# Cosine attention and a Hyena gate: k and v on 112 partitions of five tokens, and the last output rows of two batches in one tile

## The chip, the cores and the metric

The kernel runs on one core of a Trainium2 chip, in one launch. The metric is device time in microseconds (us): the median of several executions, beside one execution that a hardware profiler recorded. Inputs and outputs lie in device memory in fp32; inside, most tiles are fp16 with sums in fp32.

Engines are named as in the profile: PE (TensorE, matrix products) with its weight loads PEld, DVE (VectorE), ACT (ScalarE), POOL (GpSimd) and SP (SyncE, which here only issues DMA transfers). Each engine has a queue of its own and works it off in order; engines wait for each other through semaphores.

## The reference, cut to what matters

```python
# q, k, v: (8, 8, 576, 64) = batch, heads, sequence, head_dim
theta = pi/2 * arange(S) / S
phi(x) = concat(relu(x) * cos(theta), relu(x) * sin(theta))      # along head_dim
kv  = einsum('bhsf,bhsd->bhfd', phi(k), v)
z   = phi(k).sum(axis=2)
num = einsum('bhsf,bhfd->bhsd', phi(q), kv)
den = einsum('bhsf,bhf->bhs', phi(q), z)[..., None] + 1e-6
x   = (num / den).transpose(0, 2, 1, 3).reshape(B, S, 512)

x1, x2, x3 = split(x @ w_proj, 3)                                # w_proj (512, 1536)
conv = irfft(rfft(x2, axis=1) * rfft(filter)[None], n=S)          # filter (576, 512)
out  = (x1 * conv * x3) @ w_out                                  # w_out (512, 512), fp32
```

Attention needs sums over all 576 tokens of a head, in any order: `kv` and `z` do not depend on which token lies in which partition, as long as `k`, `v` and the angle columns agree. The output product, by contrast, needs its rows in a known order, since they are stored to their places.

## The kernel before, in words

**Tiling.** 576 is 4.5 x 128, so the tokens of a batch are dealt over 128 partitions and five columns (`NJ = 5`). `load_rows` (L156) does it with two transfers: tokens 0 to 511 go as four consecutive ones to each of 128 partitions, a run of 1 KB (L158), and the last 64 tokens as one each to partitions 0 to 63, a run of 256 B (L163). In the fifth column partitions 64 to 127 hold nothing; they are set to zero once per buffer. There are six raw buffers (`raw_buf`), used in turn by q, k and v of each batch: buffer (3 b + 0, 1 or 2) modulo 6. So 1 and 4 hold k, 2 and 5 hold v, 0 and 3 hold q. `step_pad` (L234, words `pad0` to `pad5`) zeroes their empty parts on DVE; `step_cols` (L242, word `cols`) does it for two more buffers, `k32` and `v32`.

**Loads.** `step_load` (L167, words `Lq`, `Lk`, `Lv`) issues them on POOL's queue and converts to fp16 on the way. The first four heads of k and v of batch 0 come in fp32 over SP's queue instead (`step_load32`, L174, words `Sk`, `Sv`). A word with a tilde, `~Lq3.1`, makes the load wait for the newest DVE instruction and the newest DMA transpose ahead of it in the plan (`hold`, L148).

**Attention, per batch.** `pk` (L505) makes phi(k) in ten instructions per batch or half batch, one for each column and for cosine and sine, each on ACT (L514) or DVE (L111). Its scales are the columns `ccol` and `scol`, cosine and sine of the angle of the token in each place, which `step_cols` makes from an index tile `s4_i` (L205). `pq` (L519) makes phi(q) with the cosine divided out, so that only one column `tcol` (the tangent) is needed; `epsc` is the matching small term. `va` (L539) copies v beside a column of ones. `kv` (L556, matmul L563) sums over the partitions and, in five accumulating matmuls per head, over the columns. `qt` (L573) turns phi(q): by PE for batches 0 and 1, by a DMA transpose on SP's queue from batch 2 on (L577). `num` (L600, matmul L606) multiplies by `kv`, and DVE divides (`rcp`, `att`).

**Gate, per batch.** `fx` (L629) takes a Fourier-like step of the attention result; `xt` (L659) turns that result, from batch 3 on by one DMA transpose on SP's queue (L660); `pr` (L676, matmul L680) projects to x2 in the frequency domain, and its evictions from PSUM (the accumulator memory) are the `x2f` instructions; `dft` (L701) and `mul` (L718) apply the filter; `ga` and `gb` (L730, matmul L736) are the projections to x1 and x3; `g` (L751) multiplies those two; `inv` (L765, matmuls L770 and L774) goes back to time.

**The end of a batch.** `y` (L786) adds and subtracts halves and multiplies by `g`. A step `y3.0.2` treats two of the four channel blocks (`NC = 4`) of batch 3, from block 0. Its last instruction writes `ye`, the gated values of the last 64 rows (L811 to L817); a batch that runs in two such steps has written `ye` after the second, and one that runs in more after the last. `out` (L837) multiplies by `w_out`. Groups 0 and 1 are two tiles of 128 rows each, matmul L824, one eviction of 128x1024 (`os`) and two stores (L850). Group 2 is the last 64 rows: to use all 128 output partitions, `out_tile` computes the two column halves into partitions 0 to 63 and 64 to 127, in two matmuls of 64x256 for each channel block (L829); `left` (L853) evicts 128x256 on ACT and stores the two halves on SP's queue (L858). The last batch goes by `end` (L863) in single tiles.

**What sets the order.** Nothing is scheduled automatically. One long string of words, the plan (L905 to L987), is carried out word by word while the program is built. A word names a step, its batch and its part; a step is a generator that yields after each piece, and every occurrence of its word emits one more piece, `*3` three of them. `'a` and `'v` put a piece on ACT or DVE. Each engine executes its share of what the plan emits, in the plan's order. For `out*.2` the pieces are: the matmuls; the eviction; the two stores.

PSUM is used through `unit`, a pool of four buffers taken in turn. The tiles around the end of a batch have `y` and `ye` two buffers each, `os` three and `os4` one.

Where the words of the last rows stand in the plan before (each `...` leaves out other words):

```
... fx3.0 out0.2 ... y1.0.2 ... pr4.0 ... out1.2*2 pr4.2 out1.2 ...
... y2.0.2 ... fx5.3 fx5.2 out2.2 fx5.3 ... y3.0.2 gb5.1 ga4.3 out3.0 ... inv5.1 out3.2 qt7.2 ...
... dft7.1'v dft7.0 xt7 dft7.2 out5.1 ga7.0 inv6.3 dft7.2'v gb7.0 out4.2 ... gb7.0 out5.2 mul7 ...
```

Of the kernel before, what the change touches and what calls it, by code (L numbers as in the profile page):

```python
# [17 lines left out]
def kernel(  # L18
# [41 lines left out]
    NM = NC * 128  # L60

# [104 lines left out]

    def step_load(nm):  # L167
        def load(b, half):
            raw_t[(b, nm)] = raw_buf[(3 * b + "qkv".index(nm)) % len(raw_buf)]
            load_rows(nc.gpsimd, raw_t[(b, nm)], {"q": q, "k": k, "v": v}[nm], b, at(half))  # L170
            yield
        return load

    def step_load32(nm):  # L174
        def load(b, half):
            load_rows(nc.sync, k32 if nm == "k" else v32, k if nm == "k" else v, b, at(half))
            yield
        return load
# [26 lines left out]
    def step_iota(part):  # L205
        if part == 0:
            iota("s4_i", [128, NJ], lambda t: [
                (t[:, 0:4], [[1, 4]], 0, 4), (t[0:64, 4:5], [[1, 1]], NM, 1),
                (t[64:128, 4:5], [[1, 1]], 0, 1),
            ])  # L210
            yield
            return
# [21 lines left out]
    def step_pad(i):  # L234
        nc.vector.memset(raw_buf[i][64:128, :, 4 * D : 5 * D], 0.0)
        yield
# [5 lines left out]
    def step_cols():  # L242
        nc.vector.memset(warm, 0.0)
        nc.vector.memset(half_pi, PI / 2.0)
        for r in (k32, v32):
            nc.vector.memset(r[64:128, :, 4 * D : 5 * D], 0.0)
        yield
        nc.scalar.activation(
            out=ccol, in_=cc["s4_i"], func=AF.Sin, scale=-(PI / 2.0) / S, bias=half_pi
        )  # L250
        nc.scalar.activation(out=scol, in_=cc["s4_i"], func=AF.Sin, scale=(PI / 2.0) / S)
        yield
# [5 lines left out]
        nc.vector.reciprocal(out=epsc, in_=ccol)  # L258
        yield
        nc.vector.tensor_tensor(out=tcol, in0=epsc, in1=scol, op=AL.mult)  # L260
# [244 lines left out]
    def step_pk(b, half):  # L505
# [4 lines left out]
        for j in range(NJ):  # L510
            for x, col in enumerate((ccol, scol)):
                dst, src, c = kp_t[b][:, j, hs, x], rw[:, hs, ds(j * D, D)], col[:, j : j + 1]
# [26 lines left out]
    def step_va(b, x):  # L539
        n = 2 if b == 0 else 4  # L540
        hs = slice(n * x, n * x + n)
        ev(
            va_buf[b % 2][:, hs, :, 0:D],
            (v32 if b == 0 and x < 2 else raw_t[(b, "v")])[:, hs].rearrange(
                "p h (j d) -> p h j d", j=NJ
            ),
        )
        yield
# [7 lines left out]
    def step_kv(b, half):  # L556
# [3 lines left out]
        for g in range(hv.start, hv.stop):  # L560
            for h in range(4 * g, 4 * g + 4):
                for j in range(NJ):
                    nc.tensor.matmul(  # L563
                        u[:, g, ds((h % 4) * 65, 65)], kp[:, j, h].rearrange("p a b -> p (a b)"),
                        va[:, h, j, 0:65], start=(j == 0), stop=(j == NJ - 1),
                    )
# [219 lines left out]
    def step_y(b, c, n):  # L786
# [24 lines left out]
        if "ye" not in moe[b]:  # L811
            moe[b]["ye"] = late["p"].tile([128, NC, 64], FP16, tag="ye", bufs=2, name=f"ye{b}")
        tt(
            out=moe[b]["ye"][:, c : c + n].rearrange("p c (a t) -> p c a t", t=4),
# [5 lines left out]
    def out_tile(b, t, dst, cs):  # L820
        y = moe[b]["y"]
        for c in cs:
            if t < 4:
# [3 lines left out]
                continue  # L827
            for hf in range(2):
                nc.tensor.matmul(  # L829
                    dst[ds(64 * hf, 64), 0 : DM // 2], moe[b]["ye"][:, c],  # L830
# [22 lines left out]
    def left(b, u):  # L853
        os_ = late["p"].tile([128, DM // 2], FP32, tag="os4", bufs=1, name=f"os{b}_4")
# [35 lines left out]
    def run(plan, **batch):  # L890
# [27 lines left out]
        tf'v pk1.2*4 qt1.0 va1.0'v kv1.2 va1.1'v kv1.2 th kv1.2 qt1.1 g0.0.2 qt1.0'v th
        ~Lq3.1 tf qt1.0'v qt1.1'v qt1.2 qt1.1'v qt1.2 ~Lk3.0 qt1.2 num1.0*3 tf pr0.1 th
        num1.1 num1.0 num1.2 g0.2.2 num1.1 tf ~Lq3.0 num1.2 num1.1 pr0.1 tf ti pr0.0 num1.2  # L920
        num1.1 qt1.3 num1.2 pr0.0 pr0.2 qt1.3 dft0.0 feo0 pr0.2 dft0.0 feo1 h0 qt1.3'v xp1.0
        ti xp1.0 pq2.2 fx1.1 pq2.2 h0'v h1 ~Lv2.2 pq2.2 xp1.0 pq2.2 pk2.2 xp1.0'v pk2.2
        pk2.2'a h0 fx1.1 pk2.2 num1.3*3 pq2.2 num1.3 pq2.2 qt2.3 h2 qt2.0 fx1.2 h1 pk2.2 h1
        pk2.2 xp1.1 fx1.3 xp1.1 ~Lk3.1 ~Lq4.1 ~Lv3.1 h2 fx1.2 xp1.1'v fx1.3 xp1.1'v fx1.0
        pk2.2*2 dft0.1 dft0.1'v ~Lo dft0.2 ga1.0 fx1.0 dft0.2 mul0 ti mul0 pr1.0 pr1.2 ti*2
        mul0 ga1.0 mul0 pr1.1 pr1.1'v pr1.0 ga1.0 inv0.1 inv0.0 ~Lq4.0 ti pk2.2 late pr1.2
        dft1.2 dft1.0 dft1.2'v inv0.1 dft1.1 pk2.2 inv0.0 inv0.2 va2.0'v dft1.0 kv2.2 pq3.2
        va2.1'v inv0.3 kv2.2 y0.0.2 ~Lk4.1 y0.0.2 dft1.1 inv0.2 ga1.2*2 mul1 gb1.2 mul1
        qt2.1 kv2.2 num2.0 ~Lv3.0 qt2.2 num2.0 inv0.3 num2.1 pq3.2'a ga1.2 gb1.2 ~Lv4.0
        num2.1 num2.0 num2.1 num2.0 num2.1 gb1.3*2 mul1*2 gb1.2 gb1.1*2 pq3.2'a pq3.2 gb1.3  # L930
        pq3.2'a ga1.1 pk3.2 gb1.1 num2.2 ~Lk4.0 num2.2*3 y0.0.2 ga1.1 y0.0.2 fx2.1 y0.2.2
        ga1.1 y0.2.2 gb1.0*2 pk3.2'a fx2.1 inv1.1 fx2.2 pk3.2 gb1.0 inv1.1 fx2.2 ga1.3
        y0.2.2 ga1.3 inv1.0 inv1.0'v ga1.3 xp2.0 num2.3*3 xp2.0*3 num2.3 pk3.2 inv1.3*2
        y0.0.2 inv1.2*2 fx2.0*2 fx2.3*2 g1.0.2 ga2.0 xp2.1*2 pr2.0 xp2.1*2 pq3.2 ga2.0
        y0.2.2 qt3.0 va3.0'v y1.0.2 pk3.2 pk3.2'a*2 pk3.2 y0.2.2 pk3.2'a pq4.2 pr2.1 ga2.0
        qt3.2 pq4.2 out0.0 pr2.2 pr2.1 pr2.0 out0.0 dft2.1 y1.0.2 dft2.0 ~Lq5.0 va3.1'v
        y1.0.2 ~Lq5.1 ~Lv4.1 y1.0.2 pk3.2 ~Lv5.0 qt3.1 y1.2.2*2 pr2.2'v dft2.1 y1.2.2 dft2.2
        kv3.2*2 y1.0.2 gb2.1 y0.2.2 gb2.1 dft2.0 g1.2.2 y0.0.2 pq4.2'a ~Lv5.1 qt3.3 dft2.2'v
        kv3.2 gb2.0*2 mul2*2 num3.0*4 ~Lk5.0 gb2.1 gb2.0 gb2.3 pk4.2'a gb2.3*2 ~Lk5.1 out0.2
        ga2.2*2 fx3.0 out0.2 pq4.2'a ga2.1 mul2*2 ga2.2 fx3.0 num3.1*2 num3.2*2 pk4.2'a  # L940
# [78 lines left out]
```

## Time and profile before

| | |
|---|---|
| time, median of 3 executions | 223.5 us (222.74 to 224.11) |
| the profiled execution: its own time | 224.69 us |
| the same, span from first to last instruction | 222.9 us |
| mean granted PE clock in it | 0.983 |
| read from memory, written | 33.69 MB, 9.44 MB (193 GB/s over the span) |
| DMA packets, and those under 512 B | 90907, 58944 |

The page gives the span once more in 40 slices of 5.57 us, in tenths of the slice:

```profile
PE   7388989999999999999999999799999999999990
...
DVE  7998999989999989989999997889888797589930
```

The largest groups of instructions:

| group | count | busy us | mean ns |
|---|---|---|---|
| PE, gate projections, L736 | 512 | 71.2 | 286 |
| PE, x2 projection, L680 | 160 | 34.6 | 381 |
| PE, output rows, L824 | 128 | 30.1 | 379 |
| DVE, `att` from `num` and `rcp`, L116 | 32 | 26.0 | 819 |
| ACT, `os` from `out` (groups 0 and 1, last rows), L138 | 24 | 18.3 | 767 |
| POOL, loads of q, k and v, L158 | 40 | 32.2 | about 804 |

How to read it: busy time is a sum over instructions, and matmuls overlap, so the mean of one is longer than the pace at which they follow each other. An idle time of an engine is put down to the instruction or transfer that ended it ("releaser"). In rows of a stage the columns are the stretch in us, its length, then for PE, PEld, DVE, ACT and POOL the busy time and in brackets the instructions, then the granted PE clock, the mean share of DMA engines in use and the GB/s they moved. In rows of the timeline they are the start, the busy time from first to last of the instructions put together, the engine (with a q for its DMA queue), line and operation, what is written and read, the count, and in square brackets the idle time before and what ended it.

### The profile page before, as it was taken

How to read it: one execution, taken by the hardware profiler on the slowest of the kernel's cores; microseconds unless marked ns; L12 is line 12 of the kernel's file. 1: busy time of each engine (PE TensorE's matmuls, PEld its weight loads, DVE VectorE, ACT ScalarE, POOL GpSimd, SP SyncE). 2: the span in 40 equal slices, each digit the busy share in tenths (PEclk: the TensorE clock that was granted, in tenths of full speed). 3: DMA queues.
4: the chain of work that ended last, by engine and by line, in shares of the span. 5: the costliest groups of instructions: out<-in, count | busy, mean ns of one | idle time of the engine just before them, and what ended most of it. 6: DMA issues, size and time to landing. Idle time of an engine off the chain costs nothing.

```text
span 222.9 us, 5869 instructions
## 1 busy us (share of the span) xinstructions
PE 207.7 (93%) x2316; PEld 142.8 (64%) x2316; DVE 194.7 (87%) x473; ACT 170.7 (77%) x275; POOL 65.5 (29%) x105
## 2 busy tenths in 40 slices
PE   7388989999999999999999999799999999999990
PEld 2176776574888476756686667476876667477630
DVE  7998999989999989989999997889888797589930
ACT  4796989998898999888784975877787736476651
POOL 8892456213962096003500184002200000000000
PEclk9979999999999999999999999999999999999996
DMA  5999999999999999999999999997999940823084
GB/s 170 190 186 192 191 209 193 175 138 210 144 189 184 173 161 182 169 195 163 170 157 194 200 199 182 146 300 156 110 177 149 326 132 3 197 94 138 22 258 165
DMA packets 90907, 38.39 MB, mean 172 GB/s; under 512 B 58944, under 2 KB 86592, under 8 KB 90880
## 3 DMA queue, kind: packets, MB, share of 16 engines
q0 software_dynamic: 38944, 16.26, 59.8%
q1 hardware_dynamic: 51568, 21.17, 46.0%
q10 hardware_dynamic: 368, 0.59, 0.7%
q8 instruction: 18, 0.29, 0.5%
q14 instruction: 9, 0.07, 0.1%
HBM read 33.69 MB, written 9.44 MB: 193 GB/s over the span
## 4 chain that ended last, share of the span: by engine, by line
PE 67%; DVE 14%; DMA 10%; ACT 3%; issue 2%; POOL 2%; ACTq 0%; DVEq 0%; POOLq 0%
PE x L736 22%; PE x L680 11%; PE out L824 10%; DMA xt<-att 4%; PE kv L563 4%; PE num L606 4%; PE dft L711 3%; PE fx L634 3%; DMA out_dram<-os 3%; DMA raw<-in_q_dram 3%; PE inv L770 3%; PE inv L774 2%; DVE kp L111 2%; DVE yf L116 2%; DVE qp L111 2%
## 5 line engine op out<-in xcount | busy, mean ns | idle before, releaser
L736 PE MATMUL x<-xt,wp 128*128 128x288 f16 x512 | 71.2, 286 | 0.6 <-DMA xt<-att 0.3
L736 PEld LDWEIGHTS <-wp 128*128 128x128 f16 x512 | 47.9, 98 | 15.8 <-issue 2.8
L680 PE MATMUL x<-wp,fx 128*128 128x512 f16 (+1 forms) x160 | 34.6, 381 | 0.0
L824 PE MATMUL out<-wo,y 128*128 128x512 f16 x128 | 30.1, 379 | 0.0
L138 ACT ACTIVATE os<-out 128x1024 f32<-128x1024 f32 (+2 forms) x24 | 18.3, 767 | 12.5 <-PE out L824 10.1
L116 DVE TENSOR_TENSOR att<-num,rcp 128x640 f16<-128x640 f32 x32 | 26.0, 819 | 0.6
L680 PEld LDWEIGHTS <-fx 128*128 128x128 f16 (+1 forms) x160 | 13.6, 100 | 15.0 <-issue 2.1
L138 ACT CAST x0s<-x 128x576 f16<-128x576 f32 x27 | 17.2, 641 | 6.0 <-PE x L736 5.1
L138 ACT CAST x2s<-x 128x576 f16<-128x576 f32 x28 | 17.8, 639 | 4.8 <-PE x L736 4.7
L138 ACT ACTIVATE x2f<-x 128x1024 f16<-128x1024 f32 (+1 forms) x18 | 16.2, 903 | 6.6 <-PE x L680 5.6
L158 POOL DMA_DIRECT2D raw<-in_q_dram x14 | 11.2, 797 | 31.4 <-ACT x0s L138 18.2
L824 PEld LDWEIGHTS <-y 128*128 128x128 f16 x128 | 12.1, 98 | 12.6 <-issue 0.4
L138 ACT CAST fx<-fx 128x576 f16<-128x576 f32 x29 | 17.8, 648 | 1.8 <-PE fx L640 1.5
L138 ACT CAST eq<-inv 128x576 f16<-128x576 f32 x26 | 16.0, 648 | 3.9 <-PE inv L774 3.3
L158 POOL DMA_DIRECT2D raw<-in_k_dram x13 | 10.5, 811 | 27.0 <-DVE rcp L617 14.6
L770 PE MATMUL inv<-itab,yf 128*128 128x144 f16 x128 | 16.9, 226 | 1.2 <-ACT x2f L138 0.9
L158 POOL DMA_DIRECT2D raw<-in_v_dram x13 | 10.5, 805 | 21.8 <-DVE rcp L116 17.3
L774 PE MATMUL inv<-itl,yf 128*128 128x288 f16 x64 | 16.8, 286 | 0.0
L563 PE MATMUL kv<-va,kp 128*128 128x65 f16 x320 | 12.4, 193 | 4.0 <-DVE va L134 3.8
L563 PEld LDWEIGHTS <-kp 128*128 128x128 f16 x320 | 11.6, 98 | 5.8 <-ACT kp L514 4.0
L606 PEld LDWEIGHTS <-qpt 128*128 128x128 f16 x320 | 13.0, 98 | 3.6 <-issue 0.9
L606 PE MATMUL num<-kvs,qpt 128*128 128x65 f16 x320 | 14.3, 194 | 0.9 <-ACT qpt L138 0.5
(163 smaller groups left out, 432.8 us busy)
## 6 DMA issues: line engine op xcount, KB each, us to landing
out_dram<-os SPq DMA_DIRECT2D x30, 256.0 KB, 3.2
raw<-in_q_dram POOLq DMA_DIRECT2D x12, 256.0 KB, 6.9
raw<-in_k_dram POOLq DMA_DIRECT2D x11, 256.0 KB, 7.2
raw<-in_v_dram POOLq DMA_DIRECT2D x11, 256.0 KB, 6.5
wp<-in_moe_w_proj_dram POOLq DMA_DIRECT2D x3, 512.0 KB, 8.6
raw<-in_q_dram POOLq DMA_DIRECT2D x2, 512.0 KB, 12.1
raw<-in_k_dram POOLq DMA_DIRECT2D x2, 512.0 KB, 13.3
raw<-in_v_dram POOLq DMA_DIRECT2D x2, 512.0 KB, 10.5
```

What stands on the lines that cost most here:

```text
L111: last_dve[0] = nc.vector.tensor_scalar(out=out, in0=in0, scalar1=s1, scalar2=s2, op0=op0, **({"op1": op1} if op1 else {}))
L116: last_dve[0] = nc.vector.tensor_tensor(out=out, in0=in0, in1=in1, op=op)
L138: return nc.scalar.copy(out=out, in_=in_) if mul is None else nc.scalar.mul(out=out, in_=in_, mul=mul)
L158: first = queue.dma_start(out=rw[:, to, 0 : 4 * D], in_=src[b, hs, 0:NM].rearrange("h (p j) d -> p h (j d)", j=4),)
L563: nc.tensor.matmul(u[:, g, ds((h % 4) * 65, 65)], kp[:, j, h].rearrange("p a b -> p (a b)"), va[:, h, j, 0:65], start=(j == 0), stop=(j == ...
L606: nc.tensor.matmul(u[:, hh, ds(t * 65, 65)], qpt_buf[:, h, ds(t * 128, 128)], kvs[:, h // 4, ds((h % 4) * 65, 65)], start=True, stop=True,)
L634: nc.tensor.matmul(uf[:, ds(256 * t, 144)], att[:, c, t], fm.rearrange("p v a -> p (v a)"), start=(t % 2 == 0), stop=False,)
L680: nc.tensor.matmul(dst, fx[:, c, ds(128 * ch, n)], wp16[:, c, ds(DM, DM)], start=(c == cs[0]), stop=(c == cs[-1]),)
L736: nc.tensor.matmul(u[:, hf, 0:HS], wp16[:, i, ds(w * DM + c * 128, 128)], xt[:, i, ds(HS * hf, HS)], start=(i == 0), stop=(i == NC - 1),)
L770: nc.tensor.matmul(u[:, comp, ds(par * QS, QS)], yf[:, comp, ds(par * DM + c * 128, 128)], itab[:, par + 4 * comp], start=(par == 0), stop ...
L774: nc.tensor.matmul(u[:, comp, 0:HS], yf[:, comp, 2 * DM : NF], itl[:, c, comp].rearrange("p a b -> p (a b)"), start=False, stop=True,)
L824: nc.tensor.matmul(dst, y[:, c, ds(QS * t, 128)], wo16[:, c], start=(c == 0), stop=(c == NC - 1),)
```

## The change

**k and v are dealt anew; q is not.** A new function loads k and v, for POOL's loads and for the fp32 ones on SP: tokens 0 to 559 as five consecutive ones on each of 112 partitions (`KP = 112`, a run of 1,280 B), and tokens 560 to 575 as one each on partitions 112 to 127. Column 0 is then full on 128 partitions, and columns 1 to 4 on 112. `pk` and `kv` use that many rows (`KJ`). In partitions 112 to 127 columns 1 to 4 of k and v are read by no matmul, so the memsets of k's buffers go (`pad1`, `pad4`, and those of `k32` and `v32`). v's buffers are still copied whole by `va`, so the unused part is filled once, by a transfer on POOL's queue that brings some of v's own values (`pad2`, `pad5`). The two copies from `v32` take 112 rows, and a second small instruction each copies column 0 of partitions 96 to 127.

The angle of each token's place now differs between k and q. Two more index tiles are made on POOL, `k_i` (5 p + j) and `k1_i` (448 + p + j). Their minimum `kn`, made on DVE, is the token number: 5 p + j up to partition 111, and 448 + p from 112 on in column 0. `ccol` and `scol` come from `kn`; two further sines, `cq` and `sq`, serve `tcol` and `epsc`.

**Last rows of two batches.** `ye` gets two places in its tile, `[128, NC, 2, 64]`. Batches 0 and 1, 2 and 3, 4 and 5 share one tile (`BP = 6`); the last 64 rows of both are computed together in four matmuls of 128x512, evicted in one instruction of 128x512, and stored in two transfers of 64x512, one for each batch. Batches 6 and 7 stay as they were.

**The plan.** The words `out0.2`, `out2.2` and `out4.2` are gone. `out1.2`, `out3.2` and `out5.2` are emitted as `*3` in one place each. `pad1` and `pad4` are gone, `pad2` stands behind `Lv0.1` on POOL, `pad5` behind `Lw1`. All other words keep their order.

```diff
+    BP = B - 2
+    KP = 112
+    KJ = (128,) + (KP,) * (NJ - 1)
...
+    def load_runs(queue, rw, src, b, hs):
+        to = slice(0, rw.shape[1]) if rw.shape[1] < NH else hs
+        hold(queue.dma_start(
+            out=rw[0:KP, to], in_=src[b, hs, 0 : KP * NJ].rearrange("h (p j) d -> p h (j d)", j=NJ)
+        ))
+        queue.dma_start(
+            out=rw[KP:128, to, 0:D], in_=src[b, hs, KP * NJ : S].rearrange("h p d -> p h d")
+        )
...
-            load_rows(nc.gpsimd, raw_t[(b, nm)], {"q": q, "k": k, "v": v}[nm], b, at(half))
+            (load_rows if nm == "q" else load_runs)(nc.gpsimd, raw_t[(b, nm)], {"q": q, "k": k, "v": v}[nm], b, at(half))
...
-            load_rows(nc.sync, k32 if nm == "k" else v32, k if nm == "k" else v, b, at(half))
+            load_runs(nc.sync, k32 if nm == "k" else v32, k if nm == "k" else v, b, at(half))
...
+            iota("k_i", [128, NJ], lambda t: [(t, [[1, NJ]], 0, NJ)])
+            iota("k1_i", [128, NJ], lambda t: [(t, [[1, NJ]], 4 * KP, 1)])
...
     def step_pad(i):
+        if i in (2, 5):
+            nc.gpsimd.dma_start(
+                out=raw_buf[i][KP:128, :, D:], in_=v[0, :, 0:64].rearrange("h (p j) d -> p h (j d)", j=NJ - 1)
+            )
+            yield
+            return
         nc.vector.memset(raw_buf[i][64:128, :, 4 * D : 5 * D], 0.0)
...
-        for r in (k32, v32):
-            nc.vector.memset(r[64:128, :, 4 * D : 5 * D], 0.0)
-        yield
-        nc.scalar.activation(
-            out=ccol, in_=cc["s4_i"], func=AF.Sin, scale=-(PI / 2.0) / S, bias=half_pi
-        )
-        nc.scalar.activation(out=scol, in_=cc["s4_i"], func=AF.Sin, scale=(PI / 2.0) / S)
-        yield
+        kn = small("kn", NJ)
+        tt(kn, cc["k_i"], cc["k1_i"], AL.min)
+        yield
+        cq, sq = small("cq", NJ), small("sq", NJ)
+        for n, co, si in ((kn, ccol, scol), (cc["s4_i"], cq, sq)):
+            nc.scalar.activation(out=co, in_=n, func=AF.Sin, scale=-(PI / 2.0) / S, bias=half_pi)
+            nc.scalar.activation(out=si, in_=n, func=AF.Sin, scale=(PI / 2.0) / S)
+            yield
...
-                dst, src, c = kp_t[b][:, j, hs, x], rw[:, hs, ds(j * D, D)], col[:, j : j + 1]
+                dst, src, c = kp_t[b][0 : KJ[j], j, hs, x], rw[0 : KJ[j], hs, ds(j * D, D)], col[0 : KJ[j], j : j + 1]
...
+        early = b == 0 and x < 2
+        src = (v32 if early else raw_t[(b, "v")])[:, hs].rearrange("p h (j d) -> p h j d", j=NJ)
+        dst, n = va_buf[b % 2][:, hs, :, 0:D], KP if early else 128
+        ev(dst[0:n], src[0:n])
+        if early:
+            ev(dst[96:128, :, 0], src[96:128, :, 0])
...
-                        u[:, g, ds((h % 4) * 65, 65)], kp[:, j, h].rearrange("p a b -> p (a b)"),
-                        va[:, h, j, 0:65], start=(j == 0), stop=(j == NJ - 1),
+                        u[:, g, ds((h % 4) * 65, 65)], kp[0 : KJ[j], j, h].rearrange("p a b -> p (a b)"),
+                        va[0 : KJ[j], h, j, 0:65], start=(j == 0), stop=(j == NJ - 1),
...
-            moe[b]["ye"] = late["p"].tile([128, NC, 64], FP16, tag="ye", bufs=2, name=f"ye{b}")
+            if b < BP and "ye" in moe.get(b ^ 1, {}):
+                moe[b]["ye"] = moe[b ^ 1]["ye"]
+            else:
+                moe[b]["ye"] = late["p"].tile([128, NC, 2, 64], FP16, tag="ye", bufs=2, name=f"ye{b}")
...
+            if b < BP:
+                nc.tensor.matmul(
+                    dst, moe[b]["ye"][:, c].rearrange("p b n -> p (b n)"), wo16[:, c],
+                    start=(c == 0), stop=(c == NC - 1),
+                )
+                continue
...
-        os_ = late["p"].tile([128, DM // 2], FP32, tag="os4", bufs=1, name=f"os{b}_4")
+        os_ = late["p"].tile([128, DM], FP32, tag="os4", bufs=1, name=f"os{b}_4")
+        if b < BP:
+            ev(os_, u[:, 0], OUTSC)
+            yield
+            for x in range(2):
+                nc.sync.dma_start(out=out[b - 1 + x, NM:S], in_=os_[ds(64 * x, 64)])
+            yield
+            return
```

The three places of the last rows in the plan after, with the words beside them:

```
... num4.0 y1.0.2 out1.2*3 pq5.2'a gb3.1 num4.1 ... pq5.2'a qt4.3 num4.1 ...
... ga5.0 qt6.1 out3.0 mul5 gb4.3 pk7.2'a pk7.2 pk7.2'a y3.0.2 out3.2*3 gb5.1 ga4.3 out3.0 ... qt6.2 ... qt6.3 ...
... inv6.2 pr7.0 out5.1'v y4.0.2 y5.0.2 out5.2*3 y6.0.2*4 pr7.2 pr7.1 dft7.1 ... xt7 dft7.2 ...
```

## The prediction

> **What bounds the kernel now.** The page's head, then PE over stages, then the timeline around each place the plan touches.
>
> ```profile
> span 222.9 us, 5869 instructions
> ...
> PE 207.7 (93%) x2316; PEld 142.8 (64%) x2316; DVE 194.7 (87%) x473; ACT 170.7 (77%) x275; POOL 65.5 (29%) x105
> ...
> PE 67%; DVE 14%; DMA 10%; ACT 3%; issue 2%; POOL 2%; ACTq 0%; DVEq 0%; POOLq 0%
> ```
>
> PE carries two thirds of the chain that ended last. Busy time by stage (us of PE, PEld, DVE, ACT, POOL):
>
> ```profile
> 20.00:30.00 10.00, 9.68 (x91) 7.58 (x89) 9.46 (x30) 8.69 (x18) 3.69 (x6) 1.00 1.53 192
> ...
> 30.00:40.00 10.00, 9.37 (x140) 6.66 (x141) 9.96 (x28) 9.18 (x15) 6.48 (x7) 1.00 1.41 199
> ...
> 147.00:170.00 23.00, 23.00 (x252) 17.03 (x250) 20.53 (x46) 17.77 (x28) 2.73 (x4) 1.00 0.94 172
> ...
> 170.00:190.00 20.00, 20.00 (x233) 14.25 (x232) 16.09 (x32) 12.16 (x19) 0.00 (x0) 1.00 0.60 153
> ```
>
> Up to 70 us DVE is full (95 to 99%) and shares the chain with ACT and PE. From 70 to 210 us PE is never idle but for 1.5 us at 136 to 147, and its pieces in the chain run at 0.216 us per 512-column matmul (1.73 for eight). So a PE wait put into this stage is lost for good, and a DVE or ACT instruction saved there is worth nothing. After 210 us comes a tail of output transfers (PE 7.05 busy of 13).
>
> **What the Trainium skill says.** "TensorE: Matmul & The Clock Gate", Part 1: architectural detail: ScalarE and VectorE queues are strict first in, first out; PE may only pull weight loads forward. The trace agrees: ACT stands 2.41 us ahead of 191.79 in DVE's waits and nothing overtakes. "DMA: Bandwidth & Descriptors", Anatomy of one DMA: a semaphore wait happens on the issuing sequencer before dispatch. Here SP's queue shows it: waits of up to 8.4 us for `att` before the transposes of L660. The same page, Why a DMA increments its semaphore by 16: 112 and 16 partitions both divide into 16 engines; the trace of before has no such shape. The clock gate page, Part 1: a window of about 3.4 us without enough PE work halves the clock. The trace agrees, after PE's gap from 6.49 to 9.72 us:
>
> ```profile
> 8.00:9.00 1.00, 0.00 (x0) 0.00 (x0) 0.97 (x8) 0.80 (x2) 0.82 (x2) 1.00 1.39 174
> ...
> 12.00:13.00 1.00, 1.00 (x13) 1.00 (x11) 1.00 (x6) 0.85 (x1) 1.00 (x2) 0.50 1.58 183
> ```
>
> The clock is 0.50 from about 10.8 to 14.0: 3.2 us at half pace, 1.6 us of PE work.
>
> **Part 1, loads.** Bytes are equal (576 KB per head group of four, in fp32). Tail rows fall from 64 to 16 per head. Is DMA bound by rows? In 12 to 20 us 355 of 2203 packets are under 512 B and 191 GB/s move; in 20 to 30 us 1634 of 4588, and 192 GB/s. So bytes bind: 0, between -1 (k32 and v32 come by SP, whose 256 B rows ran at 160 to 195 GB/s at 4 us) and +0.5. POOL gains two iotas (0.14 each) ahead of the first q load, which is on the chain (5.79 us to landing, DVE then idle 0.44 at 11.20): +0.3. ACT gains two sines (0.2 each, before k lands at 4.71: hidden) and one small v copy; DVE gains `kn` (0.15, while it waits for iotas) and a small v copy (at most 0.2, inside the 0.44). `pad2` is a ninth POOL transfer: eight may be outstanding (POOL waits for the transfer eight earlier at 9.62), so it goes at 9.6 and lands behind v, near 14.8, where ACT copies `va` at 14.31: 0 to +0.7, mostly absorbed by ACT's 0.83 us idle at 17.86. It also moves the three projection loads and everything behind them on POOL by about 0.7; wp2 landed 19.5, is read after 20.4. `pad5` is read at 31.2: hidden. Off DVE go six memsets: four before 2.4 us (1.09, then DVE waits for iotas instead: 0) and two in the full stage at 21.05 and 21.73 (0.27 each): -0.54 to 0, I take -0.3. Contraction over 112 rows: the 96-row matmuls of L479 take 380 ns like the 128-row ones, so 0. **Sum of part 1: 0 (-1.5 to +1).**
>
> **Part 2, last rows, as work.** Six groups of eight L829 matmuls go (0.56 us each in the chain, one 0.44: 3.24); three groups of four 128x512 come (4 x 0.216 = 0.86: 2.59): -0.7. ACT: 6 x 0.386 against 3 x 0.597, -0.5, off the path. SP issues six fewer transfers at 0.59: off the path. `ye` is written with a stride: 15 x 0.36, taken as unchanged (0 to +0.1 each, DVE).
>
> **Part 3, where the steps stand.** Each engine executes its share of the plan in the plan's order. `out1.2`, `out3.2`, `out5.2` run matmul, eviction and stores as one lump (`*3`), directly behind the words that write `ye`. Before, those three steps stood dozens of words apart. Everything behind the lump on ACT and SP waits for it.
>
> *Pair 4/5.* The plan before had `xt7` ahead of the last-row stores; now the stores of `out5.2` stand ahead of it on SP.
>
> ```profile
> 188.22 3.17 SPq L660 DMA_TRANSPOSE xt<-att  x1
> ...
> 195.19 1.02 ACT L138 ACTIVATE x2f<-x 128x1024 f16<-128x1024 f32 x1 [0.64 <-PE x L680]
> ...
> 195.58 0.62 PE L680 MATMUL x<-wp,fx 128*64 128x512 f16 x4
> ...
> 196.03 0.60 PE L829 MATMUL out<-wo,ye 128*64 128x256 f16 x8
> ...
> 197.55 1.13 SPq L858 DMA_DIRECT2D out_dram<-os  x2
> ...
> 197.66 1.15 PE L736 MATMUL x<-xt,wp 128*128 128x288 f16 x8
> ```
>
> `out5.2`'s matmuls take the place at 195.58 and end at 195.58 + 3 x 0.216 + 0.379 = 196.6; eviction 0.60: 197.25; two stores issued 1.13: 198.4; only then can `xt7` go, 5.0 us to landing (its own time here): 203.4. The gate matmul that reads `xt7` ran at 197.66. PE's own work to there is now 0.86 + 0.45 + 0.12 + 1.09, so it stands at 198.1 and waits 5.3 us. Beneath it a second wait is hidden: the eviction of `pr7.1` (195.19) now comes behind the lump's, at 197.25 to 198.2, and `dft7.1` waits 1.2 us for it. Queued behind the gates: `mul7`, `inv7`, the whole tail. **+5.3 (4 to 7).**
>
> *Pair 2/3.* `out3.2` comes right behind `out3.0`'s matmuls:
>
> ```profile
> 149.95 1.89 PE L824 MATMUL out<-wo,y 128*128 128x512 f16 x8
> ...
> 151.68 2.12 PE L736 MATMUL x<-xt,wp 128*128 128x288 f16 x16
> ...
> 154.02 0.37 DVE L116 TENSOR_TENSOR ye<-y,g 128x128 f16<-128x128 f16 x1
> ```
>
> PE is there at 151.68, the last `ye` is written at 154.39, and DVE has been busy without a gap since 145.6: PE waits 2.7. DVE then waits for `num6`, so nothing is caught up. Behind it on SP stand `qt6.2` and `qt6.3` (issued from 149 to 153 before): matmuls done 155.5, eviction 156.1, stores 157.3, first transpose landed at +3.8: 161.1, read at about 161.6; the next is on the edge: +0.5 (0 to 2). **+3.2 (2.4 to 5).**
>
> *Pair 0/1.* PE is at the lump at 103.20, the last `ye` ends at 103.38: +0.2. On SP the lump holds up `qt4.3`:
>
> ```profile
> 102.28 1.36 SPq L577 DMA_TRANSPOSE qpt<-qp  x1
> ...
> 103.69 0.75 POOL L158 DMA_DIRECT2D raw<-in_k_dram  x1 [14.20 <-DVE rcp L617]
> ...
> 109.55 2.03 SPq L577 DMA_TRANSPOSE qpt<-qp  x1
> ```
>
> Matmuls done 104.5, eviction 105.1, stores 106.3 to 107.2 (two took 2.09 at 100.10). Now it falls into the load burst that starts at 103.69: landing takes 3.5 us in quiet and 9.6 in the burst (the two transposes above), so 110 to 116, where `num4.3` reads it at about 109.6: I take 2.0 (0.2 to 6). **+2.2.**
>
> *Clock.* Each wait can fill a gate window: at most 1.6 each; pair 4/5 (4 us without a break) 1.4, the others 0.3 each: **+2.0 (0 to 4.8).**
>
> **Sum.** 0 - 0.3 - 0.7 + 5.3 + 3.2 + 2.2 + 2.0 = 11.7 us. Against the profiled execution: span 222.9 to 234.6, its own time 224.69 to 236.4. The median of the runs, 223.5, lies 1.2 below that time, so **235.2 us**.
>
> **Rivals.** *Only the DVE wait counts.* If SP's blocked transposes land in time after all (they are short and the tail has 6 us of PE idle), what is left is 2.7 + 1.2 + 0.2 - 1.0 = 3.1: 226.6. For: landing of 3.5 us in quiet. Against: `xt7` has no spare at 198.4. *Faster.* The six memsets (-0.5 in the full stage), the PE work (-0.7) and fewer short rows in the first 10 us (-1) count in full, and the waits don't: 221.3. It decides if the three waits together are below 2.2 us, which needs `xt7` landed by about 200, thus issued by 195, before its predecessor's matmuls have begun. That is only possible if SP's order is not the plan's. *The loads don't spread.* Were 112 rows served by fewer engines, bytes would bind harder: with 14 engines 16/14 of the load time in a stage that is byte bound until 35 us, some +2 on top: 237.
>
> **Numbers.** Forecast (all three queues) 0.78; only the DVE wait 0.11; loads don't spread 0.02; faster, or all of it a wash, 0.09. Faster by over 1% 0.05, within 1% 0.07, slower 0.88; 1%, 2.2 us, is about what a measurement of this kernel tells from no change. Range: from the low ends (-1.5 - 1 + 4 + 2.4 + 0.4 + 0.5 = 5) to the highs held together in part (+17): 228 to 241.
>
> **What would show it.** PE idle before the first gate of batch 7, ended by DMA `xt<-att`, with `xt` issued behind two stores; PE idle of 2 to 3 us before `out<-wo,ye` near 150 us, ended by DVE `ye`; `qpt` transposes near 107 us issued right after two stores; a clock of 0.50 after the longest gap; DVE without memsets at 21 us; load rows fewer, bytes as before. It is wrong if `xt7` is issued before the stores of `out5.2`, or if PE shows no gap over 1 us after 70 us.

## The result, and the profile after

| | before | after |
|---|---|---|
| median | 223.53 us (222.74 to 224.11, 4 runs) | 250.94 us (247.1 to 253.5, 4 runs) |
| ratio of times | | 1.111, 95% interval 1.100 to 1.121 |
| profiled execution: span, mean PE clock | 222.9 us, 0.983 | 247.6 us, 0.947 |

The kernel is 11% slower, about 25 us; the prediction said 11.7. Runs more than 1.5% above the fastest of their kernel are left out of the ratios here and below (two of these four), so a ratio can be a little less than the quotient of two medians. The span grew by 24.7 us, which agrees with the ratio, and it is what the account below explains.

The page's head, engine totals and chain, after:

```profile
span 247.6 us, 5790 instructions
...
PE 215.7 (87%) x2280; PEld 145.1 (59%) x2280; DVE 193.9 (78%) x469; ACT 170.9 (69%) x275; POOL 62.7 (25%) x109
...
PE 62%; DMA 19%; DVE 12%; ACT 2%; POOL 2%; issue 1%; DVEq 0%; POOLq 0%; ACTq 0%
```

PE runs 36 matmuls fewer and yet is busy 8 us longer, most of it the same work at a lower clock (below). The busy times of DVE, ACT and POOL are within 3 us of those before. In the chain DMA has gone from 10 to 19%.

What PE waited for after 60 us, by the view of waits (total us, times, longest):

```profile
PE num L626 <- DMA qpt<-qp: 7.9, 2, 6.0
PE x L756 <- DMA xt<-att: 4.8, 1, 4.8
PE out L854 <- DVE ye L119: 3.0, 1, 3.0
PE fx L654 <- DVE att L119: 0.9, 2, 0.7
PE dft L731 <- ACT x2f L141: 0.5, 1, 0.5
```

The first three stand at the places of the pairs of last rows: of the two waits for `qpt`, 6.0 us come at pair 0/1 and 1.8 us at pair 2/3. Up to there the two traces run side by side: at 86 us the changed kernel is 0.3 us late.

**Pair 0/1.** POOL's loads, SP's issues and PE, from the timeline after:

```profile
103.63 0.71 POOL L172 DMA_DIRECT2D raw<-in_k_dram  x1 [14.11 <-DVE rcp L119]
...
103.79 1.04 PE L854 MATMUL out<-wo,ye 128*128 128x512 f16 x4
...
105.53 1.19 SPq L890 DMA_DIRECT2D out_dram<-os  x2
...
106.81 3.10 SPq L597 DMA_TRANSPOSE qpt<-qp  x1
...
109.96 1.09 SPq L881 DMA_DIRECT2D out_dram<-os  x2
...
116.13 0.73 PE L626 MATMUL num<-kvs,qpt 128*128 128x65 f16 x10 [6.03 <-DMA qpt<-qp]
```

The transpose is issued 1.3 us behind the pair's stores and 3 us after the burst of loads began at 103.63. It lands 9.3 us later, and PE stands still for 6.0 us. Before, it was issued at 102.28 and PE needed it at 108.50.

**Pair 2/3 and pair 4/5**, PE and SP:

```profile
163.47 1.89 PE L854 MATMUL out<-wo,ye 128*128 128x512 f16 x4 [2.98 <-DVE ye L119]
...
175.36 0.48 PE L626 MATMUL num<-kvs,qpt 128*128 128x65 f16 x10 [1.82 <-DMA qpt<-qp]
...
212.89 1.14 SPq L890 DMA_DIRECT2D out_dram<-os  x2
214.13 3.88 SPq L680 DMA_TRANSPOSE xt<-att  x1
...
219.95 2.10 PE L756 MATMUL x<-xt,wp 128*128 128x288 f16 x8 [4.79 <-DMA xt<-att]
```

PE waits 2.98 us for the last `ye`, then 1.82 us for a transpose that SP issued behind the pair's stores; and at the third pair 4.79 us for `xt` of batch 7, which stands directly behind two stores.

**The clock** after each gap, by stretches of the windows view (the value after POOL's is the mean clock of the stretch):

```profile
114.00:116.00 2.00, 0.00 (x0) 0.00 (x0) 0.00 (x0) 0.00 (x0) 0.00 (x0) 0.83 1.34 256
...
118.00:120.00 2.00, 2.00 (x6) 0.70 (x5) 1.68 (x2) 0.00 (x0) 0.00 (x0) 0.50 0.53 113
...
122.00:124.00 2.00, 2.00 (x23) 1.78 (x22) 1.76 (x4) 1.18 (x2) 0.00 (x0) 0.96 0.90 170
...
163.00:166.00 3.00, 2.53 (x8) 1.16 (x9) 0.41 (x2) 0.60 (x2) 1.14 (x2) 0.52 0.00 0
...
217.00:219.00 2.00, 0.00 (x0) 0.00 (x0) 0.00 (x0) 0.00 (x0) 0.00 (x0) 0.68 0.92 205
219.00:222.00 3.00, 2.05 (x10) 1.34 (x11) 0.00 (x0) 0.00 (x0) 0.00 (x0) 0.50 1.09 384
222.00:225.00 3.00, 3.00 (x18) 2.11 (x16) 2.66 (x3) 0.75 (x2) 0.00 (x0) 0.58 0.50 178
```

A mean of 0.83 over 2 us is 0.7 us at half clock, so the half clock began at 115.3; read in the same way it ended at 122.1, after 6.8 us. At the third gap it ran from 217.7 to 224.5, again 6.8 us, and at the second, by finer stretches, from 163.1 to 166.5, 3.4 us.

To account for all of it, the same PE instruction can be looked up in both traces:

| PE instruction | before | after | later by | what was added since the row above |
|---|---|---|---|---|
| gates just behind pair 0/1 | 103.20 | 104.66 | 1.5 | 0.3 from the start, 0.3 wait for `ye`, 0.9 own matmuls |
| last `num` of batch 4 | 108.50 | 116.13 | 7.6 | 6.0 transpose |
| `fx` of batch 4 | 111.51 | 121.99 | 10.5 | 2.8 half clock |
| gates at 146 us before | 146.22 | 154.85 | 8.6 | -1.9: gaps of before that close, last rows not computed here |
| gates just behind pair 2/3 | 151.68 | 165.15 | 13.5 | 3.0 wait for `ye`, 0.9 own matmuls, 0.8 half clock |
| `num` of batch 6 | 159.23 | 175.36 | 16.1 | 0.7 half clock, 1.8 transpose, 0.2 rest |
| last `x2` projection of batch 7 | 195.58 | 212.16 | 16.6 | 0.9 own matmuls of pair 4/5, 0.4 of it gained back |
| first gates of batch 7 | 197.66 | 219.95 | 22.3 | 4.8 `xt`, 0.5 `x2f`, 0.4 rest |
| gates of batch 7 | 200.12 | 224.64 | 24.5 | 2.2 half clock |
| end of span | 222.9 | 247.6 | 24.7 | |

Waits at the three places 16.4 us (0.3 + 6.0 + 3.0 + 1.8 + 4.8 + 0.5), half clock 6.5 us, the rest 1.8. These are readings of one execution of each kernel; the experiments test them.

### The profile page after: what moved, and what is told of

Same layout as the page of the kernel before. It is cut to its first block, busy times and chain, and to the rows that moved or that the text cites. A ratio compares the mean times of both kernels' runs of the same rounds, so it can differ in the third digit from the quotient of the medians.

```text
span 247.6 us, 5790 instructions
## 1 busy us (share of the span) xinstructions
PE 215.7 (87%) x2280; PEld 145.1 (59%) x2280; DVE 193.9 (78%) x469; ACT 170.9 (69%) x275; POOL 62.7 (25%) x109
## 4 chain that ended last, share of the span: by engine, by line
PE 62%; DMA 19%; DVE 12%; ACT 2%; POOL 2%; issue 1%; DVEq 0%; POOLq 0%; ACTq 0%
PE x L756 19%; PE x L700 11%; PE out L849 10%; DMA qpt<-qp 6%; DMA raw<-in_v_dram 4%; DMA wp<-in_moe_w_proj_dram 3%; PE num L626 3%; PE fx L654 3%; PE inv L790 3%; PE inv L794 3%; PE kv L583 3%; DMA xt<-att 2%; DMA raw<-in_q_dram 2%; PE dft L731 2%; DVE yf L119 2%; DVE xf L119 2%
## 5 line engine op out<-in xcount | busy, mean ns | idle before, releaser
L756 PE MATMUL x<-xt,wp 128*128 128x288 f16 x512 | 74.4, 295 | 5.3 <-DMA xt<-att 4.8
L756 PEld LDWEIGHTS <-wp 128*128 128x128 f16 x512 | 49.7, 101 | 22.7 <-DMA xt<-att 5.0
L141 ACT ACTIVATE os<-out 128x1024 f32<-128x1024 f32 (+2 forms) x21 | 17.6, 851 | 27.8 <-PE out L849 20.1
L849 PE MATMUL out<-wo,y 128*128 128x512 f16 x128 | 31.8, 395 | 0.0
L700 PEld LDWEIGHTS <-fx 128*128 128x128 f16 (+1 forms) x160 | 13.3, 100 | 16.1 <-issue 2.7
L626 PE MATMUL num<-kvs,qpt 128*128 128x65 f16 x320 | 14.9, 199 | 8.5 <-DMA qpt<-qp 7.9
L849 PEld LDWEIGHTS <-y 128*128 128x128 f16 x128 | 12.5, 101 | 13.5 <-issue 2.0
L626 PEld LDWEIGHTS <-qpt 128*128 128x128 f16 x320 | 13.5, 101 | 11.6 <-DMA qpt<-qp 8.5
L119 DVE TENSOR_TENSOR rcp<-num,epsc 128x10 f32<-128x10 f32 x32 | 5.1, 165 | 19.2 <-PE num L626 18.5
L172 POOL DMA_DIRECT2D raw<-in_v_dram x13 | 9.7, 749 | 32.4 <-issue 21.3
L583 PE MATMUL kv<-va,kp 112*128 112x65 f16 (+1 forms) x320 | 12.9, 198 | 4.5 <-ACT qp L552 3.7
L172 POOL DMA_DIRECT2D raw<-in_k_dram x13 | 9.7, 748 | 27.1 <-DVE rcp L119 15.1
```

What stands on the lines that cost most here:

```text
L119: last_dve[0] = nc.vector.tensor_tensor(out=out, in0=in0, in1=in1, op=op)
L141: return nc.scalar.copy(out=out, in_=in_) if mul is None else nc.scalar.mul(out=out, in_=in_, mul=mul)
L172: hold(queue.dma_start(out=rw[0:KP, to], in_=src[b, hs, 0 : KP * NJ].rearrange("h (p j) d -> p h (j d)", j=NJ)))
L583: nc.tensor.matmul(u[:, g, ds((h % 4) * 65, 65)], kp[0 : KJ[j], j, h].rearrange("p a b -> p (a b)"), va[0 : KJ[j], h, j, 0:65], start=(j = ...
L626: nc.tensor.matmul(u[:, hh, ds(t * 65, 65)], qpt_buf[:, h, ds(t * 128, 128)], kvs[:, h // 4, ds((h % 4) * 65, 65)], start=True, stop=True,)
L700: nc.tensor.matmul(dst, fx[:, c, ds(128 * ch, n)], wp16[:, c, ds(DM, DM)], start=(c == cs[0]), stop=(c == cs[-1]),)
```

## The experiments

The theory, A: all of the loss comes from where the three steps stand, that is from what SP, ACT and PE execute behind them. Rivals: the new deal of k and v costs (B); the burst of loads or ACT's order matters, not SP's (C, D). Times are medians; ratios are to the kernel before.

### One part alone

`loads_only`: the new deal of k and v, with the last rows and their words as before. `rows_only`: pairs and their places, k and v as before.

> Only the new deal of k and v (with its sines, copies and moved fills); the last rows as before the change. Theory A (all of the loss comes from where the three steps of the last rows stand): 223 to 224.5 us, PE gaps after 70 us as in the kernel before, two half-clock windows or fewer at the start. Rival B (the new deal lands later or bunches the transfers so that the transposes near 107 us come late): at least 5 us of the 27 stay, so above 228 us.

> Only the last rows in pairs, with their new places; k and v dealt as before. Theory A: 247 to 252 us, with the three PE gaps of the changed kernel (about 6.0, 3.0 and 4.8 us). Rival B: below 244 us, above all the gap near 110 us shorter than 4 us.

| | median | ratio |
|---|---|---|
| loads_only | 223.71 us | 1.001 (0.998 to 1.004) |
| rows_only | 250.77 us | 1.109 (1.101 to 1.117) |

The new loads cost and bring nothing; the last rows carry the whole loss. Rival B falls.

### Pair 0/1: the transpose first

```diff
-num4.0 y1.0.2 out1.2*3 pq5.2'a ... pq5.2'a qt4.3 num4.1
+num4.0 y1.0.2 qt4.3 out1.2*3 pq5.2'a ... pq5.2'a num4.1
```

> The changed kernel with one transpose, the last one of phi(q) of batch 4, issued on SP before the stores of the first pair instead of behind them. Theory A: it lands in 3.5 to 4.5 us, the PE gap of 6.0 us and the half clock behind it (2.6 us) go, so 8.5 us less than the changed kernel: about 241 us. Rival C (the burst of loads is what is late, and the transpose would be late wherever it stood; or the next transpose, of batch 5, takes its place): less than 4 us gained, above 246 us.

246.40 us, ratio 1.101 (1.094 to 1.108): by the ratios 2.2 us less than the changed kernel, with intervals that overlap. Theory A's 8.5 us did not come, and the time is the one that rival C had named. C's reason for it does not hold: PE no longer waits for this transpose or for the next. The 6.0 us gap is gone, and its successor is in the timeline (SP, ACT, PE of this kernel):

```profile
106.78 1.11 SPq L881 DMA_DIRECT2D out_dram<-os  x2
...
116.66 1.02 ACT L141 ACTIVATE os<-out 128x1024 f32<-128x1024 f32 x1 [5.14 <-DMA out_dram<-os]
...
117.73 1.69 PE L756 MATMUL x<-xt,wp 128*128 128x288 f16 x7 [3.81 <-ACT os L141]
```

The two stores of a 128-row tile, which stand behind the pair's stores too, are issued at 106.78, inside the burst, and the second lands near 116.6. The eviction at 116.66 needs their `os` buffer, one of three, and ACT stands 5.1 us for it; PE then waits 3.8 us for the PSUM buffer. In the changed kernel this eviction came only at 120.31, behind PE's wait for the transpose, so the second wait did not show. Before the change these stores were issued at 103.69.

### Pair 0/1: only the stores later, and only the burst later

```diff
# stores01_later
-... y1.0.2 out1.2*3 pq5.2'a ... num4.3 out0.0 out1.1*2
+... y1.0.2 out1.2*2 pq5.2'a ... num4.3 out0.0 out1.2 out1.1*2
# loads6_later: SP's order as in the changed kernel
-... y1.2.2 ~Lk6.0 ~Lq6.0 kv4.2*2 ... dft3.2 ~Lk6.1 ... num4.1 ~Lq6.1 pq5.2'a ... qt4.3 num4.1
+... y1.2.2 kv4.2*2 ... dft3.2 ... num4.1 pq5.2'a ... qt4.3 ~Lk6.0 ~Lq6.0 ~Lk6.1 ~Lq6.1 num4.1
```

> The changed kernel with only the two stores of the first pair issued later on SP, behind the transpose of phi(q) of batch 4 and behind the next two stores of 128-row tiles, which the eviction of 128x1024 near 113 us needs landed. Theory E (the lump on SP does harm in two steps: first through the transpose, and where that is mended through an output buffer that comes back late): both go, 7.5 to 9.5 us less than the changed kernel, so 240 to 243 us, and no PE gap over 1 us between 103 and 125 us. Rival: no more than with the transpose alone moved, 246 us.

> The changed kernel with SP's order kept (stores of the first pair ahead of the transpose), but the four load groups of batch 6 put behind that transpose in the plan, so that they wait for it. If the burst of loads is what makes the transpose land 9.3 us after its issue, it now lands in 3.4 to 5 us and PE waits under 1 us for it: the changed kernel less 5 to 8 us, 242 to 245 us, if batch 6 does not wait for its loads. If SP's order alone is the cost, the transpose lands late all the same and the time stays at 249 to 251 us.

| | median | ratio | less than the changed kernel, by ratio |
|---|---|---|---|
| stores01_later | 239.55 us | 1.068 (1.059 to 1.077) | 9.5 us |
| loads6_later | 244.08 us | 1.088 (1.077 to 1.098) | 5.2 us |

With only the pair's stores moved, nothing is left of pair 0/1 in PE's waits after 60 us; what is left belongs to the other two pairs:

```profile
PE x L756 <- DMA xt<-att: 4.3, 1, 4.3
PE out L854 <- DVE ye L119: 3.0, 1, 3.0
```

With SP's order kept and the burst moved, SP and POOL read as follows, with PE's wait for the transposes from the view of waits:

```profile
106.12 1.18 SPq L890 DMA_DIRECT2D out_dram<-os  x2
107.40 1.58 SPq L597 DMA_TRANSPOSE qpt<-qp  x1
109.02 1.06 SPq L881 DMA_DIRECT2D out_dram<-os  x2
```

```profile
111.85 0.71 POOL L172 DMA_DIRECT2D raw<-in_k_dram  x1 [21.10 <-ACT qp L552]
```

```profile
PE num L626 <- DMA qpt<-qp: 0.9, 2, 0.6
```

The transpose is issued even later than in the changed kernel, 107.40 against 106.81, and PE waits 0.6 us for it, not 6.0. So both are needed for the loss: SP pushes the transpose 4.5 us back (102.28 to 106.81) and the stores behind it 3.1 us or more (103.69 to 106.78 in `qt43_first`), and there they meet the burst. This kernel gains less than the other because the moved burst meets the next transpose on SP, `xt` of batch 4: issued at 113.97, it lands 13.3 us later and PE waits 1.6 us for it. The view of waits counts it together with the 4.7 us of pair 4/5:

```profile
PE x L756 <- DMA xt<-att: 6.3, 2, 4.7
```

### Pair 2/3 and pair 4/5

```diff
# pair23_later
-pk7.2'a y3.0.2 out3.2*3 gb5.1 ...
+pk7.2'a y3.0.2 gb5.1 ... inv5.1 out3.2 qt7.2 ... pr6.2 out3.2 kv7.2*2 ... mul6 out3.2 out3.0
# xt7_first
-y5.0.2 out5.2*3 y6.0.2*4 ... xt7 dft7.2
+y5.0.2 out5.2*2 y6.0.2*4 ... xt7 out5.2 dft7.2
```

> The changed kernel with the second pair's matmuls, eviction and stores at the three places that they had for batch 3 before the change. Theory A: the 3.0 us wait for ye, the 1.8 us wait for the transpose behind the stores and a half-clock window (1.0 us) go: 5 to 6.5 us less, 244 to 246 us. Rival (PE only waits elsewhere: the burst or DVE holds it up a little later): under 2.5 us gained.

> The changed kernel with the two stores of the third pair behind the last attention transpose on SP, matmuls and eviction left where they are. Theory A: the 4.8 us gap before the gates of batch 7 goes; PE still waits 1.2 us for the x2f eviction behind the last rows' one on ACT; with the half clock gone too, 5 to 7 us less than the changed kernel: 243 to 246 us. Rival D (the eviction order on ACT decides, the transpose is hidden by the tail): less than 2 us gained.

| | median | ratio | less than the changed kernel, by ratio |
|---|---|---|---|
| pair23_later | 242.99 us | 1.086 (1.078 to 1.094) | 5.6 us |
| xt7_first | 245.14 us | 1.089 (1.080 to 1.098) | 4.9 us |

In the first the wait for `ye` and the 1.8 us for the transpose are gone from PE's list. This move takes away both at once, so how the two share the loss is read from the trace and was not tested. In the second, PE no longer waits for `xt`; SP and PE:

```profile
207.36 3.10 SPq L680 DMA_TRANSPOSE xt<-att  x1
216.31 1.14 SPq L890 DMA_DIRECT2D out_dram<-os  x2
```

```profile
217.25 0.39 PE L731 MATMUL dft<-x2f,fcos 128*32 128x512 f16 x2 [0.52 <-ACT x2f L141]
...
218.51 1.16 PE L756 MATMUL x<-xt,wp 128*128 128x288 f16 x8
```

The eviction order on ACT, which was left as changed, costs 0.5 us. Rival D falls. In this execution the wait at pair 0/1 was longer, though the words up to there are those of the changed kernel:

```profile
106.93 2.84 SPq L597 DMA_TRANSPOSE qpt<-qp  x1
...
117.22 0.73 PE L626 MATMUL num<-kvs,qpt 128*128 128x65 f16 x10 [7.00 <-DMA qpt<-qp]
```

The transpose landed after 10.3 us here and after 9.3 in the changed kernel: what the burst costs is not the same in these two executions.

### All together

`three_mended` makes the three moves at once. `pairs_old_places` keeps the new loads and pair tiles, with the words of each pair where batches 1, 3 and 5 had them; `rows_old_places` is the same with the old loads.

> The changed kernel with the three single moves together: the first pair's stores later on SP, the second pair at batch 3's old places, the third pair's stores behind the last attention transpose. Alone they gained 11.4, 8.0 and 5.8 us; if the three losses are independent, the sum of 25.2 comes off the changed kernel: 225 to 227 us. If mending one uncovers another behind it: above 229 us.

> The changed kernel's loads and pair tiles, with all three pairs' matmuls, evictions and stores at the places that batches 1, 3 and 5 had before the change, and none for batches 0, 2 and 4. Theory A: all three gaps go and the saved PE work is left (six groups of eight matmuls against three of four, 0.7 us): 222 to 224.5 us, the same as the kernel before or up to 0.7 us faster. Rival F (the pair tile itself costs: the strided write of ye, the wider eviction, two stores of 128 KB at once): above 226 us.

> Only the pair tiles, at the old places; k and v dealt as before the change. If the 1.5 us of the kernel with both parts come from the pairs (through the instruction transfer, or otherwise), it is at 225 to 226 us here too. If they come from the two parts together or from the loads: 224 us or less.

| | median | ratio |
|---|---|---|
| three_mended | 226.76 us | 1.015 (1.011 to 1.019) |
| pairs_old_places | 225.41 us | 1.007 (1.005 to 1.009) |
| rows_old_places | 224.98 us | 1.006 (1.004 to 1.008) |

Three moves of words, with every tile and matmul of the change left in, take away 21.5 of the 24.8 us by the ratios, against 20.0 for the sum of the three alone: within the intervals the losses are independent, and theory A holds for all but some 3 us. Of PE's waits at the three places only the 0.5 us for `x2f` is left in the trace of `three_mended` (the 0.7 us for `att` stand at 86 us in the changed kernel too), and its clock is full from 60 us to the tail:

```profile
PE fx L654 <- DVE att L119: 0.8, 2, 0.7
PE dft L731 <- ACT x2f L141: 0.5, 1, 0.5
```

Some 1.5 us of the remaining 3.3 stand in `pairs_old_places` as well, where 222 to 224.5 us had been expected; the others were not traced further. So the pair tile at good places is no gain: 0.6 to 0.7% slower than before. PE had taken the saving (at 196 us it was 0.5 us ahead of the kernel before) and lost it in the tail. There SP's four stores of 128-row tiles take longer to issue in `pairs_old_places` than in the next kernel, whose line comes second:

```profile
211.60 3.56 SPq L881 DMA_DIRECT2D out_dram<-os  x4
```

```profile
211.28 2.53 SPq L882 DMA_DIRECT2D out_dram<-os  x4
```

One of the four took 1.45 us instead of 0.43. In the same stretch, 212 to 216 us, one transfer of the instruction queue runs, 16 KB by the trace, which before fell at 207.3 us. The view of DMA queues has it (packets, MB, share of the 16 engines):

```profile
q8 instruction: 1, 0.02, 1.8%
```

The page counts 18 such transfers; that PE's instruction count sets where they fall was the idea of the last two runs.

```diff
-                u[:, x % 2], warm[:, 0:128], warm, ...          # word warm0.12
+            w = warm if x < 12 else warm[:, 0:8]
+                u[:, x % 2, 0 : w.shape[1]], warm[:, 0:128], w, ...   # word warm0.48
```

> The kernel with all pairs at the old places, plus 36 tiny matmuls of 8 columns behind the twelve warm-up matmuls at the start, in PE's gap from 6.5 to 9.7 us: as many PE instructions (72 with the weight loads) as the pairs had taken away. Theory G: with the pairs at the old places the last 16 KB instruction transfer (queue q8) falls at 213.6 us, among the last stores, where a store issue takes 1.45 us instead of 0.43 us; before it fell at 207.3 us. With the count restored it falls near 207 us again and the tail is as before: 223.5 to 224.5 us against 225.4. Rival (the pair's stores or the pair tile itself cost the 1.5 us): 225 us or more.

> Control: the kernel before, with the same 36 tiny matmuls and nothing else. If they only move instruction transfers and fill a gap in which PE waits anyway: 223.2 to 224.8 us, no change. If a warm clock at the start is worth something: up to 1.6 us less, 222.3 us.

| | median | ratio |
|---|---|---|
| pairs_warm36 | 224.49 us | 1.006 (1.003 to 1.008) |
| before_warm36 | 225.07 us | 1.006 (1.003 to 1.009) |

In the trace the idea holds: the transfer is back at 207.2 us, the store takes 0.43 us, the tail is as before (the second line above). In the time it doesn't show: the control, which was to change nothing, became 0.6% slower by the extra matmuls alone, for a reason that was not found, and against this control the pairs are level (1.006 both). Whether the instruction transfer is what the pair tiles pay at the old places stays open. No version here is shown to be faster than the kernel before.

## Why the prediction was wrong

The direction, the three places, the queue and the late item at each were right; the sum was half of what came. Its terms, against the profiled execution:

| term | predicted | measured |
|---|---|---|
| loads (part 1, with the memsets) | -0.3 | none to be told (`loads_only`: 1.001); the changed kernel 0.3 late at 86 us |
| last rows as work | -0.7 | -0.5 (PE of `pairs_old_places` at 196 us) |
| pair 4/5 | 5.3 | 5.3 (4.8 + 0.5) |
| pair 2/3 | 3.2 (2.7 + 0.5) | 4.8 (3.0 + 1.8) |
| pair 0/1 | 2.2 (0.2 + 2.0) | 6.3 (0.3 + 6.0) |
| clock | 2.0 (0 to 4.8): 0.3 at 0/1, 0.3 at 2/3, 1.4 at 4/5 | 6.5: 2.8, 1.5, 2.2 |

The measured terms add up to 22.7, so 2 us of the growth of 24.7 have no term here. Part of it is the work on the last rows: its -0.5 was seen in `pairs_old_places` only. In the changed kernel the eight matmuls that are gone at 84.5 us became a wait, 0.7 us for `att` at 86.5. The prediction also seems to count the two memsets twice, once in the 0 of part 1 and once as -0.3 in the sum.

Two terms failed by their size, by about as much each.

**The first is pair 0/1: "so 110 to 116, where `num4.3` reads it at about 109.6: I take 2.0 (0.2 to 6)".** The issue came as worked out, at 106.8. The transpose landed at 116.1, at the far end, and cost 6.0. The prediction had both rows in hand, 3.5 us in quiet and 9.6 us in the burst, and had worked out that the issue falls into the burst; it then took a value near the quiet end. The row that fits the state was the right one: 106.8 + 9.6 = 116.4. It also followed only one of the two things that SP holds up there. The stores behind the transpose come late too, and `qt43_first` and `stores01_later` show what they are worth: moving the transpose alone brings 2.2 us, moving the pair's stores away 9.5.

**The second is the clock: "at most 1.6 each".** That figure came from one window in the trace of before, put at 3.2 us (by finer stretches 3.4). After the gaps of 6.0 and 4.8 us the clock stayed at half for 6.8 us, two such windows, and half of PE's busy time in them is lost: 2.8 and 2.2 us. The longer wait at pair 0/1 explains a part of this, but the ceiling itself was wrong, at pair 4/5 too. The Trainium skill bears on this on the page that the prediction used, "TensorE: Matmul & The Clock Gate", Part 1 (What's actually happening): full speed comes back only after a busy window of about 3.4 us. The trace agrees: in the 3.4 us from 115.3 and from 217.7 PE was busy for 2.6 and 1.2 us, and a second window at half clock followed; in those from 163.1 it was busy for 3.05, and full speed followed.

How much a gap costs is not set by its length. The wait for `ye` is the same in three traces (2.98, 2.99 and 3.00 us), and the half clock behind it lasts 3.4 us in the changed kernel, 6.8 in `qt43_first`, and does not come at all in `xt7_first`. The changed kernel, `qt43_first` and `xt7_first`, in windows of 3.41 us that follow the places where the clock changes in each trace:

```profile
159.70:163.11 3.41, 0.79 (x4) 0.18 (x2) 3.27 (x8) 0.97 (x2) 0.00 (x0) 1.00 0.00 0
...
163.11:166.52 3.41, 3.05 (x10) 1.49 (x11) 0.30 (x2) 1.12 (x2) 1.21 (x2) 0.50 0.09 5
```

```profile
155.46:158.88 3.42, 1.34 (x7) 0.39 (x4) 3.28 (x7) 1.52 (x3) 0.00 (x0) 1.00 0.00 0
...
158.88:162.29 3.41, 2.50 (x8) 1.14 (x9) 0.85 (x3) 0.57 (x2) 1.11 (x2) 0.50 0.00 0
```

```profile
157.64:161.05 3.41, 2.44 (x14) 1.11 (x12) 3.27 (x7) 1.87 (x3) 0.00 (x0) 1.00 0.25 46
161.05:164.46 3.41, 1.39 (x9) 0.82 (x10) 1.97 (x4) 0.31 (x1) 0.00 (x0) 1.00 0.00 0
```

In the changed kernel the half clock begins at 115.32, 163.11 and 217.72, that is 47.79 and 54.61 us apart, 14 and 16 times 3.413. In `xt7_first` the gap falls across two such windows, and PE is busy for 2.4 and 1.4 us in them; in the changed kernel it leaves 0.8 us of work in one. This grid of 3.41 us lies elsewhere in each trace, so where a gap would fall on it could not be foreseen; a range was the right form for this term, and it was too low.

**Pair 2/3** was mis-sized in its second half: "the next is on the edge: +0.5 (0 to 2)" was 1.8, inside its range. The second of the two transposes landed 5.9 us after its issue, where 3.8 had been taken. The first half, 2.7 for the wait on `ye`, was 3.0. **Pair 4/5** came out as a sum: 5.3 for the wait on `xt7` with a second one of 1.2 hidden beneath it was said, and 4.8 and 0.5 one after the other were measured. Luck has a part in that: `xt7` took 5.8 us to land, not 5.0, and PE's own work up to its first gates was 0.9 us longer than worked out, and the two nearly cancel.

Of the rivals, "only the DVE wait counts" fails: of the 16.4 us of waits 12.6 (6.0 + 1.8 + 4.8) are for transposes that stand behind stores on SP. "The loads don't spread" fails with `loads_only`. "Faster" needed the three waits together below 2.2 us; they were 16.4.

## What to carry to other kernels

Where work is merged to be done once, look at what each in-order queue executes behind its new place, all of it: the store that comes late holds a buffer, and the buffer holds an engine. Price a transfer by a row of the trace in the same traffic as at the new time of issue, and let that row decide, not the middle of the range. A move of the traffic can mend one transfer and catch another. A PE gap costs itself and then half of PE's busy time in the stretches at half clock behind it; here 16.4 us of waits brought 6.5 us more, and a gap of 3.0 us was followed by none, one or two windows of 3.4 us.

## What the runs showed of the hardware

- The same kind of transpose landed in 3.5 us in quiet, and in 9.3 us (10.3 in `xt7_first`) when it was issued 3 us into a burst of eight load transfers on POOL's queue. Two 128-row stores issued there (`qt43_first`) landed after 7.8 and 9.1 us; the median of such stores in the kernel before was 3.2 us.
- In each of the fourteen traces every stretch of half clock lasted for 3.41 us or two or three times that, the one at the end aside, which the trace cuts off. It lasted 6.8 us after PE gaps of 6.0 and 4.8 us; after a gap of 3.0 us it lasted 6.8 us, 3.4 us or nothing (`qt43_first`, the changed kernel, `xt7_first`). In the changed kernel it began 0.4 to 2.2 us before the gap had ended.
- A 16 KB transfer of the instruction queue beside the last stores went with a store issue of 1.45 us instead of 0.43 us; 36 small matmuls more at the start moved it by 6.4 us. It is no single case: in the fourteen traces all 20 store issues of more than 1.1 us overlap such a transfer, two of them in the kernel before (100.10 and 171.31 us). That it costs time in the median was not shown.
- k and v on 112 partitions by runs of five tokens, with the last 16 rows on 16 more, ran like 128 partitions by four and 64 rows: 1.001 (0.998 to 1.004).
